# Gated linear attention and a multiplicative feed-forward: heads' rows interleaved by six, GpSimd out of the gates, passes moved to ScalarE

## The chip, the cores and the metric

The kernel runs on one core of a Trainium2 chip. The core has five engines that work side by side: TensorE (PE in the profile, with its weight loads as PEld), VectorE (DVE), ScalarE (ACT), GpSimd (POOL) and SyncE (SP, which here only issues transfers). Each engine runs its own instructions in the order in which they stand in its queue. The metric is the device time of one execution in microseconds; less is better.

## The reference

Attention with complex gates: for each of 4 batches and 8 heads a state of 48 x 48 is multiplied by a gate at each of 768 steps, takes in k v', and is read by q. The result, as 3072 tokens of 384, goes through a feed-forward without an activation function.

```python
mag = np.sqrt(a_re * a_re + a_im * a_im)
scale = np.minimum(mag, 0.999) / (mag + 1e-06)
a_re_n, a_im_n = (a_re * scale, a_im * scale)
for t in range(S):
    ar, ai = (a_re_n[:, :, t, :, None], a_im_n[:, :, t, :, None])
    new_re = ar * S_re - ai * S_im
    new_im = ar * S_im + ai * S_re
    kv = np.einsum('bhd,bhe->bhde', k[:, :, t], v[:, :, t])
    S_re, S_im = (new_re + kv, new_im)
    y[:, :, t] = np.einsum('bhd,bhde->bhe', q[:, :, t], S_re)
...
a = x @ w1
b = x @ w2
h = a * b @ w3
return (h @ w_out).astype(np.float32)
```

## The kernel before, in words

The work is cut into eight units: unit u is one half (384 steps) of one batch, with all eight heads. A unit's inputs lie with 128 partitions (16 rows d by 8 heads) and three blocks f of 384 steps, so that row 16 f + d of a head is in partition 8 d + head of block f.

- `gates(u)` turns the gates into running products. Magnitude and angle are kept apart: ScalarE takes logarithms, exponentials, arctan, sine and cosine (all through `act`, L536 of the profile), VectorE scans along the steps (L575 for the magnitude, L600 for the angle), and q and k are multiplied by the magnitude's running product and by its inverse (L587, L588, on GpSimd), then by cosine and sine (L616 to L620). GpSimd also forms im / re (L551) and spreads v into a padded layout (`spread_v`, L513). L606 to L608 take whole turns off the angle by adding and subtracting a large constant, `ROUND`. Unit 0 does all this in three pieces of 384 (split), the others in one piece of 1152.
- `move` (L631) then brings K and Q to one head's layout, since a matmul needs the 96 numbers of a head (48 rows with cosine, 48 with sine) in 96 partitions: KL and QL. There are twelve moves a unit (cosine or sine, three f, K and Q), each from 128 partitions to 16. All transfers are issued from SP's queue.
- `turn` transposes K for the state (copied out of PSUM by ScalarE, L652), `scores` (L661) multiplies K by Q, `state` (L697 to L704) carries the state from block to block, `outputs` (L687) forms y.
- `ffn_ab` (L714, L718, L719) and `ffn_out` (L724, L727) do the feed-forward of the unit before. `fuse` (L805) multiplies w3 by w_out once at the start, with weights that `convert` (L744 to L748) turns from 64-bit to 32-bit floats on ScalarE and VectorE.
- `check_weights` yields "looks": 36 further transfers of weights into a single buffer, each read by two ScalarE passes (L772, L773).

TensorE's order is written out by hand: in `unit` a piece of attention of unit u alternates with a piece of feed-forward of unit u - 1. The steps of `gates(u + 1)` are taken between them, and one look a piece. On the other engines and in SP's queue a scheduler sets the order when the kernel is built, within the data's dependencies; it may bring an instruction forward past others.

Of the kernel before, what the change touches and what calls it, by code (L numbers as in the profile page):

```python
# [10 lines left out]
FP = mybir.dt.float32  # L11
# [361 lines left out]
def kernel(  # L373
# [36 lines left out]
    nc = tc.nc  # L410
# [15 lines left out]
    LO, HI = 32, D - 32  # L426
    LN_EPS = math.log(1e-6)
    PI = math.pi
    ROUND = 1.5 * 2.0 ** 23
    MIN_SQ = 1.126 ** 2  # L430
    SMALL, LARGE, STEEP, DECAY, ANGLE = 2.0 ** -7, 2.0 ** 40, 1.5, math.exp(-32.0), 50.0

# [76 lines left out]
    def spread_v(u):  # L509
        vr = g_t[u]["vr"].rearrange("p c (h two d) -> p c h two d", two=2, d=D)  # L510
        V = Vb[u % 2].rearrange("p c (h two) e -> p c h two e", two=2)
        for i, e0 in enumerate((0, 64 - D)):
            nc.gpsimd.tensor_copy(out=V[:, :, :, i, e0:e0 + D], in_=vr[:, :, :, i])  # L513

    chained = []

# [6 lines left out]
    def gates(u, split):  # L523

        b, h = divmod(u, 2)
        g = g_t.setdefault(u, {})
        A = gate_pool[u % 2].tile([P, KD, TT], FP, tag="gA", name="gA")
        R = gate_pool[u % 2].tile([P, KD, TT + UC], FP, tag="gR", name="gR")
        Z = one.tile([P, KD, TT], FP, tag="gZ", name="gZ")
        re, im, q = g["re"], g["im"], g["q"]  # L530
        K2 = g["k"]
        k, r = K2[:, :, 0:TT], R[:, :, 0:TT]
        parts = [slice(f, f + 1) for f in range(KD)] if split else [slice(0, KD)]

        def act(**kw):
            chain(nc.scalar.activation(**kw))  # L536
# [12 lines left out]
        yield
        for i, s in enumerate(parts):  # L550
            nc.gpsimd.tensor_tensor(out=im[:, s], in0=im[:, s], in1=r[:, s], op=OP.mult)  # L551
            act(out=Z[:, s], in_=re[:, s], func=AF.Relu, scale=-1.0, bias=LEAST, accum_out=st_low[:, 0, u, i:i + 1])
            act(out=Z[:, s], in_=re[:, s], func=AF.Relu, bias=MOST, accum_out=st_low[:, 1, u, i:i + 1])
        yield
        for i, s in enumerate(parts):
            nc.vector.tensor_tensor_reduce(out=Z[:, s], in0=im[:, s], in1=im[:, s], scale=1.0, scalar=0.0,
                                           op0=OP.mult, op1=OP.max, accum_out=st_tan[:, u, i:i + 1])
        yield
        for s in parts:
            act(out=Z[:, s], in_=Z[:, s], func=AF.Ln, bias=ONE)  # L560
        yield

        for s in parts:
            stt(out=A[:, s], in0=Z[:, s], scalar=0.5, in1=A[:, s], op0=OP.mult, op1=OP.add)
            act(out=Z[:, s], in_=A[:, s], func=AF.Exp, scale=-1.0, bias=EPS)
            act(out=A[:, s], in_=A[:, s], func=AF.Exp)
        yield

        for s in parts:
            ts(out=Z[:, s], in0=Z[:, s], scalar1=-1.0, scalar2=1.0, op0=OP.mult, op1=OP.add)  # L570
            ts(out=A[:, s], in0=A[:, s], scalar1=0.999, scalar2=None, op0=OP.min)
            for f in range(s.start, s.stop):
                for c in range(UC):
                    w = slice(c * C, (c + 1) * C)
                    nc.vector.tensor_tensor_scan(out=A[:, f, w], data0=A[:, f, w], data1=Z[:, f, w], initial=1.0,  # L575
                                                 op0=OP.mult, op1=OP.mult)
        yield

        for s in parts:
            act(out=r[:, s], in_=A[:, s], func=AF.Ln)  # L580
            act(out=r[:, s], in_=r[:, s], func=AF.Exp, scale=-1.0)
        yield
        for s in parts:
            tt(out=Z[:, s], in0=A[:, s], in1=r[:, s], op=OP.mult)
            stt(out=r[:, s], in0=Z[:, s], scalar=2.0, in1=r[:, s], op0=OP.subtract, op1=OP.mult, reverse0=True)
        for s in parts:
            nc.gpsimd.tensor_tensor(out=q[:, s], in0=q[:, s], in1=A[:, s], op=OP.mult)  # L587
            nc.gpsimd.tensor_tensor(out=k[:, s], in0=k[:, s], in1=r[:, s], op=OP.mult)  # L588
        for X in (R, K2):
            nc.vector.tensor_copy(out=X[:, :, TT:TT + UC], in_=ends(A, slice(0, KD)))  # L590
        nc.vector.tensor_copy(out=st_dec[:, u], in_=R[:, :, TT:TT + UC])
        spread_v(u)
        yield
        chain(nc.scalar.preload_act_table_set("trig_and_small"))
        for s in parts:
            act(out=im[:, s], in_=im[:, s], func=AF.Arctan)
        yield
        for s in parts:
            for f in range(s.start, s.stop):
                nc.vector.tensor_tensor_scan(  # L600
                    out=Z[:, f], data0=im[:, f], data1=im[:, f],
                    initial=0.0 if h == 0 else st_ang[:, u - 1, f, UC - 1:UC], op0=OP.add, op1=OP.bypass)
        nc.vector.tensor_copy(out=st_ang[:, u], in_=ends(Z, slice(0, KD)))
        yield
        for s in parts:
            ts(out=re[:, s], in0=Z[:, s], scalar1=0.5 / PI, scalar2=ROUND, op0=OP.mult, op1=OP.add)  # L606
            ts(out=re[:, s], in0=re[:, s], scalar1=ROUND, scalar2=2 * PI, op0=OP.subtract, op1=OP.mult)
            tt(out=Z[:, s], in0=Z[:, s], in1=re[:, s], op=OP.subtract)  # L608
        yield
        for s in parts:  # L610
            act(out=re[:, s], in_=Z[:, s], func=AF.Abs)
            act(out=re[:, s], in_=re[:, s], func=AF.Sin, scale=-1.0, bias=QUARTER)
            act(out=Z[:, s], in_=Z[:, s], func=AF.Sin)
        yield
        if not split:
            tt(out=r, in0=k, in1=re, op=OP.mult)  # L616
            tt(out=k, in0=k, in1=Z, op=OP.mult)
            yield
            tt(out=A, in0=q, in1=re, op=OP.mult)
            tt(out=q, in0=q, in1=Z, op=OP.mult)  # L620
        yield "move"

        KL = head_pool[u % 2].tile([2 * D, H, TT + UC], FP, tag="KL", name="KL")
        QL = head_pool[u % 2].tile([2 * D, H, TT], FP, tag="QL", name="QL")
        L_t[u] = QL, KL, R, K2

        def move(dst, src, s):
            for x in range(2):
                for f in range(KD)[s]:
                    r0 = x * D + f * DG  # L630
                    nc.sync.dma_start(out=dst[r0:r0 + DG], in_=src[x][:, f])  # L631

        for s in parts:
            if split:
                tt(out=r[:, s], in0=k[:, s], in1=re[:, s], op=OP.mult)
                tt(out=k[:, s], in0=k[:, s], in1=Z[:, s], op=OP.mult)
            move(KL, (R, K2), s)
            if split:
                tt(out=A[:, s], in0=q[:, s], in1=re[:, s], op=OP.mult)
                tt(out=q[:, s], in0=q[:, s], in1=Z[:, s], op=OP.mult)  # L640
            move(QL, (A, q), s)
        yield

    def turn(u, c, x):

        src = L_t[u][2 + x]
        if x == 0:
            KT_t[u, c] = two.tile([P, H, 2, D], FP, tag="KT", name="KT")
        tp = ps_v.tile([P, KD, C], FP, tag="v", name="tp")
        for f in range(KD):  # L650
            nc.tensor.transpose(out=tp[:, f], in_=src[:, f, c * C:(c + 1) * C], identity=ident)
        nc.scalar.copy(out=KT_t[u, c][:, :, x], in_=tp.rearrange("p f c -> p (f c)").rearrange("p (d h) -> p h d", h=H))  # L652
# [37 lines left out]
    def state(u, c):  # L690
# [3 lines left out]
        T = T_t.get((u // 2, n))  # L694
        kv = ps_v.tile([2 * D, H, 64], FP, tag="v", name="kv")
        for hd in range(H):
            nc.tensor.matmul(out=kv[:, hd], lhsT=KT[:, hd], rhs=V[:, hd], start=True, stop=True)  # L697
        rho = KL[:, :, TT + c:TT + c + 1].to_broadcast([2 * D, H, 64])
        Tn = two.tile([2 * D, H, 64], FP, tag="T", name="T")
        if T is None:  # L700
# [145 lines left out]
    def ffn(u):  # L846
        return [lambda j=j: ffn_ab(u, j) for j in range(KF)] + [lambda t=t: ffn_out(u, t) for t in range(UC)]
# [12 lines left out]
    with tc.manual_schedule(engines={mybir.EngineType.PE}):  # L860
# [106 lines left out]
```

## Time and profile before

| | before |
|---|---|
| median of 3 runs (lowest to highest) | 667.16 us (665.15 to 668.01) |
| the profiled execution's own time | 665.67 us |
| its span, first to last instruction | 663.9 us |
| mean granted TensorE clock | 0.941 |
| busy in the span: PE / PEld / DVE / ACT / POOL | 573.4 / 378.0 / 334.1 / 285.1 / 87.2 us |
| moved by DMA | 83.58 MB in 52146 packets |

Lines of groups give: line, engine, operation, output <- inputs, shapes, count | busy us, mean ns of one | idle time of the engine ahead of them, and what ended it. Lines of a timeline give: start us, duration us, engine, line, operation, count, and in brackets the idle time before, with what ended it. Busy shares are means over the whole execution; the stages differ much.

### The profile page before, as it was taken

To read this page: it belongs to the slowest core of one execution; us is meant where nothing else is said; L and a number is where in the kernel's file an instruction comes from. 1 tells how busy PE (TensorE), PEld (TensorE's weight loads), DVE (VectorE), ACT (ScalarE), POOL (GpSimd) and SP (SyncE) were. 2 spreads that over 40 slices of the span, in tenths; PEclk is the share of its full clock that TensorE was granted. 3 is DMA by queue.
4 is the path that set the end of the run, shared out by engine and by line. 5 is a ranking of instruction groups with operands and counts; after the bars stand their busy time and mean duration, and the time that the engine had idled before them with its cause. 6 is when DMAs were issued, how large, how long until landed. Compare 5 with 4: busy or idle time off the path is not lost.

```text
span 663.9 us, 8912 instructions
## 1 busy us (share of the span) xinstructions
PE 573.4 (86%) x3514; PEld 378.0 (57%) x3514; DVE 334.1 (50%) x501; ACT 285.1 (43%) x454; POOL 87.2 (13%) x57
## 2 busy tenths in 40 slices
PE   0769687966966799999984999799999999999996
PEld 0335474534743566676643676466656766766553
DVE  5999498831881387048601495138705961220110
ACT  6655275534751675177531855255316331101100
POOL 5050033001320130013000130013001300000000
PEclk9979899996969799999996999979999999999999
DMA  9977998397449637953469433951590067001001
GB/s 290 312 227 184 189 264 281 104 112 148 129 132 132 173 88 159 173 174 120 124 117 180 147 113 105 149 159 37 85 154 14 1 78 102 1 1 36 1 1 39
DMA packets 52146, 83.58 MB, mean 126 GB/s; under 512 B 4480, under 2 KB 43392, under 8 KB 52096
## 3 DMA queue, kind: packets, MB, share of 16 engines
q1 hardware_dynamic: 52096, 82.93, 55.2%
q8 instruction: 29, 0.48, 0.3%
q14 instruction: 21, 0.17, 0.1%
HBM read 59.24 MB, written 4.72 MB: 96 GB/s over the span
## 4 chain that ended last, share of the span: by engine, by line
PE 50%; DMA 20%; DVE 13%; ACT 11%; issue 4%; SPq 2%; ACTq 0%; DVEq 0%
PE m L714 25%; PE o L724 12%; DMA look<-in_w_dram 6%; PE sc L661 5%; DMA KL<-k 5%; DMA look<-in_w_out_dram 3%; DMA QL<-q 3%; PE y L687 3%; ACT gZ L536 3%; PE kv L697 2%; DVE gA L575 2%; DVE gZ L600 2%; ACT gR L536 2%; ACT look L773 1%; ACT look L772 1%
## 5 line engine op out<-in xcount | busy, mean ns | idle before, releaser
L714 PE MATMUL m<-xT,w2s 128*128 128x384 f32 x384 | 137.3, 495 | 6.8 <-ACT a L718 6.8
L714 PE MATMUL m<-xT,w1s 128*128 128x384 f32 x384 | 141.4, 506 | 1.6 <-ACT xT L688 1.6
L724 PE MATMUL o<-w3o,ab 128*128 128x384 f32 x384 | 129.4, 493 | 0.0
L719 DVE TENSOR_TENSOR ab<-m,a 128x384 f32<-128x384 f32 x64 | 35.3, 551 | 170.9 <-PE m L714 139.6
L714 PEld LDWEIGHTS m<-xT,w2s 128*128 128x128 f32 x384 | 74.0, 193 | 60.3 <-ACT a L718 8.9
L724 PEld LDWEIGHTS o<-w3o,ab 128*128 128x128 f32 x384 | 72.4, 192 | 48.2 <-issue 2.7
L714 PEld LDWEIGHTS m<-xT,w1s 128*128 128x128 f32 x384 | 72.1, 198 | 45.1 <-issue 6.0
L661 PE MATMUL sc<-QL,KL 96*128 96x128 f32 x384 | 56.9, 310 | 42.1 <-DMA look<-in_w_dram 19.4
L661 PEld LDWEIGHTS sc<-QL,KL 96*128 96x128 f32 x384 | 53.6, 220 | 49.0 <-issue 34.9
L718 ACT COPY a<-m 128x384 f32<-128x384 f32 x64 | 30.3, 474 | 96.7 <-PE m L714 93.9
L805 PE MATMUL f<-wo_s,w3s 128*128 128x384 f32 x128 | 46.9, 525 | 26.6 <-DVE wo_s L748 18.0
L662 DVE COPY_PREDICATED A<-causal,sc 128x512 f32<-128x512 int32 x48 | 34.4, 730 | 66.6 <-PE sc L661 66.4
L772 ACT ACTIVATE look<-look 128x512 f32<-128x512 f32 (+1 forms) x36 | 23.4, 651 | 74.7 <-DMA look<-in_w_dram 56.3
L805 PEld LDWEIGHTS f<-wo_s,w3s 128*128 128x128 f32 x128 | 25.7, 205 | 47.1 <-DVE wo_s L748 20.4
L551 POOL TENSOR_TENSOR im<-im,gR 128x1152 f32<-128x1152 f32 (+1 forms) x10 | 20.7, 2075 | 221.9 <-ACT gR L536 137.4
L687 PE MATMUL y<-A,V 128*32 128x128 f32 x768 | 41.8, 281 | 6.9 <-DVE A L662 5.0
L687 PEld LDWEIGHTS y<-A,V 128*32 128x32 f32 x768 | 34.2, 111 | 16.3 <-issue 10.1
L687 PE MATMUL y<-QL,T 96*32 96x128 f32 x640 | 37.1, 280 | 0.0
L587 POOL TENSOR_TENSOR q<-q,gA 128x1152 f32<-128x1152 f32 (+1 forms) x10 | 22.7, 2274 | 93.4 <-DVE gA L575 92.0
L687 PEld LDWEIGHTS y<-QL,T 96*32 96x32 f32 x640 | 32.7, 113 | 0.1
L744 ACT ACTIVATE low<-raw 128x768 int32<-128x768 uint32 (+1 forms) x20 | 20.2, 1011 | 29.3 <-DMA raw<-in_w_dram 12.7
L727 ACT COPY ot<-o 128x384 f32<-128x384 f32 x24 | 11.4, 473 | 48.3 <-PE o L724 48.3
(96 smaller groups left out, 648.6 us busy)
## 6 DMA issues: line engine op xcount, KB each, us to landing
look<-in_w_dram SPq DMA_DIRECT2D x28, 512.0 KB, 4.4
raw<-in_w_dram SPq DMA_DIRECT2D x8, 1024.0 KB, 5.7
raw<-in_w_dram SPq DMA_DIRECT2D x8, 768.0 KB, 9.7
KL<-gR SPq DMA_DIRECT2D x24, 193.5 KB, 5.8
KL<-k SPq DMA_DIRECT2D x24, 193.5 KB, 8.1
re<-in_a_re_dram SPq DMA_DIRECT2D x24, 192.0 KB, 8.4
im<-in_a_im_dram SPq DMA_DIRECT2D x24, 192.0 KB, 3.7
k<-in_k_dram SPq DMA_DIRECT2D x24, 192.0 KB, 3.2
```

Source lines behind the costliest of these rows:

```text
L536: chain(nc.scalar.activation(**kw))
L551: nc.gpsimd.tensor_tensor(out=im[:, s], in0=im[:, s], in1=r[:, s], op=OP.mult)
L587: nc.gpsimd.tensor_tensor(out=q[:, s], in0=q[:, s], in1=A[:, s], op=OP.mult)
L661: nc.tensor.matmul(out=sc[:, j], lhsT=KL[:, x * n + j, w], rhs=QL[:, x * n + j, w], start=True, stop=True)
L662: nc.vector.copy_predicated(out=A[:, x * n:(x + 1) * n], data=sc, mask=causal.rearrange("p (h t) -> p h t", h=1).to_broadcast([P, n, C]))
L687: nc.tensor.matmul(out=o, lhsT=a, rhs=b, start=s0, stop=s1)
L714: nc.tensor.matmul(out=m, lhsT=w[:, j * P // WB, f, j * P % WB:j * P % WB + P], rhs=xT_t[u][:, f], start=(f == 0), stop=(f == KD - 1))
L718: nc.scalar.copy(out=a, in_=got[0])
L719: nc.vector.tensor_tensor(out=ab_t[u][:, j], in0=got[1], in1=a, op=OP.mult)
L724: nc.tensor.matmul(out=m, lhsT=ab_t[u][:, f, t * P:(t + 1) * P], rhs=w3o[:, f], start=(f == 0), stop=(f == KF - 1))
L772: nc.scalar.activation(out=hi, in_=hi, func=AF.Square, scale=2.0 ** 15)
L805: nc.tensor.matmul(out=m, lhsT=w3_t[j][:, f], rhs=w3_t["wo"][:, f], start=(f == 0), stop=(f == KF - 1))
```

## The change

Five things are done at once.

1. `move` writes every sixth partition: row d of block f, cosine or sine x, goes to partition 6 d + 3 x + f of KL and QL, where it went to 48 x + 16 f + d. The transposed K gets the same order of its 96 columns, so ScalarE's copy into KT reads in order and writes with gaps, where it read with gaps and wrote in runs.
2. The three multiplies of the gates that GpSimd did go to VectorE, and V's two copies to ScalarE.
3. 1 - Z goes from VectorE to ScalarE, as a third pass between two Exps.
4. Whole turns are found by one ScalarE pass that writes integers, and taken off by one VectorE pass; three VectorE passes go.
5. Looks begin with unit 2's pieces in the program, not with unit 1's.

```diff
-            nc.gpsimd.tensor_copy(out=V[:, :, :, i, e0:e0 + D], in_=vr[:, :, :, i])
+            nc.scalar.copy(out=V[:, :, :, i, e0:e0 + D], in_=vr[:, :, :, i])
...
-            nc.gpsimd.tensor_tensor(out=im[:, s], in0=im[:, s], in1=r[:, s], op=OP.mult)
+            tt(out=im[:, s], in0=im[:, s], in1=r[:, s], op=OP.mult)
...
             act(out=Z[:, s], in_=A[:, s], func=AF.Exp, scale=-1.0, bias=EPS)
+            act(out=Z[:, s], in_=Z[:, s], func=AF.Copy, scale=-1.0, bias=1.0)
             act(out=A[:, s], in_=A[:, s], func=AF.Exp)
...
-            ts(out=Z[:, s], in0=Z[:, s], scalar1=-1.0, scalar2=1.0, op0=OP.mult, op1=OP.add)
...
-            nc.gpsimd.tensor_tensor(out=q[:, s], in0=q[:, s], in1=A[:, s], op=OP.mult)
-            nc.gpsimd.tensor_tensor(out=k[:, s], in0=k[:, s], in1=r[:, s], op=OP.mult)
+            tt(out=q[:, s], in0=q[:, s], in1=A[:, s], op=OP.mult)
+            tt(out=k[:, s], in0=k[:, s], in1=r[:, s], op=OP.mult)
...
-            ts(out=re[:, s], in0=Z[:, s], scalar1=0.5 / PI, scalar2=ROUND, op0=OP.mult, op1=OP.add)
-            ts(out=re[:, s], in0=re[:, s], scalar1=ROUND, scalar2=2 * PI, op0=OP.subtract, op1=OP.mult)
-            tt(out=Z[:, s], in0=Z[:, s], in1=re[:, s], op=OP.subtract)
+            n = re[:, s].bitcast(I32)
+            act(out=n, in_=Z[:, s], func=AF.Copy, scale=0.5 / PI)
+            stt(out=Z[:, s], in0=n, scalar=-2 * PI, in1=Z[:, s], op0=OP.mult, op1=OP.add)
...
-                    r0 = x * D + f * DG
-                    nc.sync.dma_start(out=dst[r0:r0 + DG], in_=src[x][:, f])
+                    nc.sync.dma_start(out=dst[x * KD + f::2 * KD], in_=src[x][:, f])
...
-            KT_t[u, c] = two.tile([P, H, 2, D], FP, tag="KT", name="KT")
+            KT_t[u, c] = two.tile([P, H, DG, 2, KD], FP, tag="KT", name="KT")
...
-        nc.scalar.copy(out=KT_t[u, c][:, :, x], in_=tp.rearrange("p f c -> p (f c)").rearrange("p (d h) -> p h d", h=H))
+        nc.scalar.copy(out=KT_t[u, c][:, :, :, x].rearrange("p h d f -> p f d h"),
+                       in_=tp.rearrange("p f (d h) -> p f d h", h=H))
...
-            unit(u, steps, rest[HEAD:] if u == 1 else ffn(u - 1), look)
+            unit(u, steps, rest[HEAD:] if u == 1 else ffn(u - 1), look if u > 1 else iter(()))
```

Three places show what the scheduler makes of it. SP's queue at the end of unit 3, with the moves of unit 4 (KL and QL; gR and k hold K with cosine and sine, gA and q hold Q), before:

```order
L482 DMA im<-in_a_im_dram 128x1x384 x3
L770 DMA look<-in_w_dram 128x1024
L631 DMA KL<-gR 16x8x387
L770 DMA look<-in_w_dram 128x1024
L631 DMA KL<-gR 16x8x387
L770 DMA look<-in_w_dram 128x1024
L631 DMA KL<-gR 16x8x387
L770 DMA look<-in_w_dram 128x1024
L631 DMA KL<-k 16x8x387 x3
L631 DMA QL<-gA 16x8x384 x3
L631 DMA QL<-q 16x8x384 x3
```

The same place in the changed kernel:

```order
L481 DMA im<-in_a_im_dram 128x1x384 x3
L769 DMA look<-in_w_dram 128x1024
L629 DMA KL<-gR 16x8x387 x3
L629 DMA KL<-k 16x8x387 x3
L629 DMA QL<-gA 16x8x384 x3
L629 DMA QL<-q 16x8x384 x3
```

The three looks between the moves are gone from here, and so are the two between unit 5's; the changed kernel has one look between unit 6's moves, where there was none.

VectorE in unit 1, with the gates of unit 2, from the magnitude's scans (L575, L574 in the changed kernel) to the angle without whole turns, before:

```order
L575 SCALAR_TENSOR_TENSOR gA<-gA,gZ 128x128 x9
L590 COPY gR<-gA 128x3x3
L590 COPY k<-gA 128x3x3
L591 COPY st_dec<-gR 128x9
L584 TENSOR_TENSOR gZ<-gA,gR 128x1152
L662 COPY_PREDICATED A_85<-causal,sc 128x512
L585 SCALAR_TENSOR_TENSOR gR<-gZ,gR 128x3x384
L662 COPY_PREDICATED A_85<-causal,sc 128x512
L600 SCALAR_TENSOR_TENSOR gZ<-im 128x384 x3
```

The same stretch in the changed kernel:

```order
L574 SCALAR_TENSOR_TENSOR gA<-gA,gZ 128x128 x9
L586 TENSOR_TENSOR q<-q,gA 128x1152
L589 COPY gR<-gA 128x3x3
L589 COPY k<-gA 128x3x3
L590 COPY st_dec<-gR 128x9
L661 COPY_PREDICATED A_85<-causal,sc 128x512
L583 TENSOR_TENSOR gZ<-gA,gR 128x1152
L661 COPY_PREDICATED A_85<-causal,sc 128x512
L584 SCALAR_TENSOR_TENSOR gR<-gZ,gR 128x3x384
L702 TENSOR_TENSOR T<-kv,T 96x512
L587 TENSOR_TENSOR k<-k,gR 128x3x384
L599 SCALAR_TENSOR_TENSOR gZ<-im 128x384 x3
```

q's multiply now follows the magnitude's scans, and k's stands ahead of the angle's scans.

ScalarE at the end of unit 0, with the second Ln and Exp of unit 1's gates (gR), before:

```order
L688 COPY xT<-y 128x3x128
L536 ACTIVATE gR<-gA 128x3x384
L744 ACTIVATE low<-raw 128x768
L536 ACTIVATE gR<-gR 128x3x384
L718 COPY a<-m 128x384
```

The same place in the changed kernel:

```order
L687 COPY xT<-y 128x3x128
L512 COPY V_87<-vr 128x12x48 x2
L535 ACTIVATE gR<-gA 128x3x384
L717 COPY a<-m 128x384
L535 ACTIVATE gR<-gR 128x3x384
```

Both copies of V for unit 2, which wait for v's landing and for unit 0's last output, stand ahead of that Ln.

More of the change, by code (lines that the diff above doesn't have):

```diff
@@ L428 @@
     PI = math.pi
-    ROUND = 1.5 * 2.0 ** 23
     MIN_SQ = 1.126 ** 2
@@ L696, in state @@
         for hd in range(H):
-            nc.tensor.matmul(out=kv[:, hd], lhsT=KT[:, hd], rhs=V[:, hd], start=True, stop=True)
+            nc.tensor.matmul(out=kv[:, hd], lhsT=KT[:, hd].rearrange("p d x f -> p (d x f)"), rhs=V[:, hd], start=True, stop=True)
         rho = KL[:, :, TT + c:TT + c + 1].to_broadcast([2 * D, H, 64])
```

## The prediction

> **What bounds the kernel now.** I read the page's first line and then TensorE's own list of waits (engine and line, what it waited for: total us, times, longest).
>
> ```profile
> span 663.9 us, 8912 instructions
> ```
>
> ```profile
> PE sc L661 <- DMA look<-in_w_dram: 19.4, 2, 9.7
> ...
> PE sc L661 <- DMA QL<-q: 17.0, 2, 11.8
> ```
>
> After the opening, TensorE waits mostly in one place: the first scores of a unit (L661), for a DMA. A score matmul reads only QL and KL, so "look" is just the transfer that landed at that moment; what is missing is the moved rows. The timeline of TensorE gives the first scores of units 0 to 7 (start, duration, idle before).
>
> ```profile
> 79.27 3.79 PE L661 MATMUL sc<-QL,KL 96*128 96x128 f32 x16 [5.19 <-DMA QL<-q]
> ...
> 155.75 3.75 PE L661 MATMUL sc<-QL,KL 96*128 96x128 f32 x16 [11.79 <-DMA QL<-q]
> ...
> 219.18 3.75 PE L661 MATMUL sc<-QL,KL 96*128 96x128 f32 x16 [9.62 <-DMA look<-in_w_dram]
> ...
> 284.85 1.95 PE L661 MATMUL sc<-QL,KL 96*128 96x128 f32 x16
> ...
> 348.54 2.20 PE L714 MATMUL m<-xT,w2s 128*128 128x384 f32 x6 [3.30 <-ACT a L718]
> ...
> 360.49 3.76 PE L661 MATMUL sc<-QL,KL 96*128 96x128 f32 x16 [9.75 <-DMA look<-in_w_dram]
> ...
> 433.07 3.75 PE L661 MATMUL sc<-QL,KL 96*128 96x128 f32 x16 [5.74 <-DMA look<-in_w_out_dram]
> 436.62 3.29 PE L714 MATMUL m<-xT,w1s 128*128 128x384 f32 x6
> 439.75 2.10 PE L714 MATMUL m<-xT,w2s 128*128 128x384 f32 x6
> ...
> 498.23 1.95 PE L661 MATMUL sc<-QL,KL 96*128 96x128 f32 x16
> ...
> 561.51 1.95 PE L661 MATMUL sc<-QL,KL 96*128 96x128 f32 x16
> ```
>
> Five of eight units start late. After such a wait the same matmuls run slow for some 3 us: 3.75 instead of 1.95, then 3.29 instead of 2.10, so a stall of this kind costs 3.0 us more than its idle time. A unit without any wait takes 561.51 - 498.23 = 63.3 us. Now the queue of SP, which issues the moves.
>
> ```profile
> 133.02 1.90 SPq L631 DMA_DIRECT2D KL<-gR  x3
> ...
> 196.25 2.10 SPq L631 DMA_DIRECT2D KL<-gR  x3
> ...
> 324.08 0.61 SPq L631 DMA_DIRECT2D KL<-gR  x1
> 326.43 0.33 SPq L770 DMA_DIRECT2D look<-in_w_dram  x1
> ...
> 340.74 1.84 SPq L631 DMA_DIRECT2D KL<-k  x3
> ```
>
> From the first move to the first score are 22.7 us (unit 1) and 22.9 (unit 2). In unit 4, three looks stand between the first moves, each waiting for its single buffer: 16.7 us pass before the fourth move. The rate, from two windows (after the busy times: granted clock, DMA share, GB/s): the first holds moves alone, the second loads from HBM in rows of about the same size.
>
> ```profile
> 144.00:155.00 11.00, 0.00 (x0) 0.00 (x0) 0.00 (x0) 0.48 (x1) 0.00 (x0) 0.72 1.10 118
> 83.00:91.00 8.00, 7.36 (x90) 6.69 (x88) 6.81 (x9) 6.93 (x11) 2.56 (x1) 0.94 1.07 330
> ```
>
> The DMA engines are full in both, but the moves get 118 GB/s against 330. Landing times of the rows KL, and of the stores to out, which read 128 partitions and write HBM:
>
> ```profile
> DMA to landing us min/median/max: 3.7/6.8/10.8
> ```
>
> ```profile
> DMA to landing us min/median/max: 1.8/3.2/12.1
> ```
>
> The same 192 KB read from all partitions can land in 1.8 us, so the read side is not what is slow. A move writes 16 neighbouring partitions; that is the suspect.
>
> **The moves (stride six).** Bounds for twelve moves of 193 KB, 2.37 MB: at 118 GB/s 20 us, as now; at 330 GB/s 7.2 us, but SP issues three in 1.90 us, so the last leaves after 7.0 us and lands no earlier than 2.8 later (estimate: 1 us above the fastest store), 9.8. I take 11.5, near the fast end, since 16 written rows would now be spread over 96. That saves 11.3 us a unit (0 to 13).
>
> [...]
>
> **Up to the first score (79.27).** VectorE is nearly full here, in pieces of 384.
>
> ```profile
> L584 DVE TENSOR_TENSOR gZ<-gA,gR 128x384 f32<-128x384 f32 x3 | 4.0, 1348 | 0.0
> ...
> L635 DVE TENSOR_TENSOR gR<-k,re 128x384 f32<-128x384 f32 x3 | 1.7, 561 | 0.0
> ...
> L570 DVE TENSOR_SCALAR gZ<-gZ 128x384 f32<-128x384 f32 x3 | 1.0, 338 | 0.0
> ```
>
> ```profile
> 32.57 2.22 DVE L575 TENSOR_TENSOR_SCAN gA<-gA,gZ 128x128 f32<-128x128 f32 x3
> ...
> 36.67 1.04 DVE L575 TENSOR_TENSOR_SCAN gA<-gA,gZ 128x128 f32<-128x128 f32 x3
> ```
>
> ```profile
> 70.51 0.56 SPq L631 DMA_DIRECT2D QL<-q  x1
> ```
>
> Added to VectorE: nine multiplies from GpSimd and three passes on n, 12 x 0.56 = 6.7 us. Removed: nine one-input passes x 0.34 and three subtractions x 0.56, 4.7. Like shapes ran at 1.35 instead of 0.56 and 2.22 instead of 1.04 while GpSimd worked; without it 3 x 0.79 + 1.2 = 3.6 go. Net -1.6. The last move landed 8.8 us after its issue behind the others; at the fastest move's 3.7 the first score comes at 70.5 - 1.6 + 3.7 = 72.6: **-7** (-2 to -9). ScalarE's six extra passes and two copies of V lie in its idle time there.
>
> **Unit 0 to 1 (76.5 us).** Prices at full width:
>
> ```profile
> L745 DVE TENSOR_SCALAR w1s<-raw 128x768 int32<-128x768 int32 x4 | 6.0, 1498 | 1.5 <-DMA raw<-in_w_dram 1.5
> ...
> L745 DVE TENSOR_SCALAR w2s<-raw 128x768 int32<-128x768 int32 x4 | 2.2, 548 | 0.0
> ```
>
> ```profile
> L652 ACT COPY KT<-tp 128x384 f32<-128x384 f32 x40 | 18.9, 476 | 29.3 <-PE tp L651 29.2
> ...
> L551 POOL TENSOR_TENSOR im<-im,gR 128x1152 f32<-128x1152 f32 x7 | 17.6, 2513 | 218.4 <-ACT gR L536 137.4 <-DMA out_dram<-ot 42.2 <-DMA q<-in_q_dram 38.7
> ...
> L616 DVE TENSOR_TENSOR gR<-k,re 128x1152 f32<-128x1152 f32 x7 | 9.5, 1359 | 12.8 <-ACT re L536 10.7 <-issue 2.1
> ...
> L536 ACT ACTIVATE im<-im 128x1152 f32<-128x1152 f32 x7 | 8.1, 1158 | 0.0
> ...
> L570 DVE TENSOR_SCALAR gZ<-gZ 128x1152 f32<-128x1152 f32 x7 | 5.3, 751 | 3.9 <-ACT gZ L536 3.9
> ```
>
> The weight passes beside GpSimd took 1.50 instead of 0.55: 3.8 us go. im: 2.51 to 1.36, -1.2. Two multiplies come onto VectorE, +2.7. 1 - Z on ScalarE between its two Exps: 1.16 for 0.75, +0.4. n: two passes and a subtraction, 2.9, become 1.16 + 1.36: -0.3. Two copies of V, 0.65 each (between 476 ns for 384 and 1158 for 1152), now stand on ScalarE ahead of the gates' second Ln: +1.3. With the moves' -11.3 this makes -12.2; I take **-11** (0 to -15), since each handover may add a little. First score of unit 1 at 137.8.
>
> **Unit 1 to 2 (63.4 us).** This interval is bound by the gates, not by TensorE: sin and cos come late, then the moves.
>
> ```profile
> 157.57 1.16 ACT L536 ACTIVATE gA<-re 128x1152 f32<-128x1152 f32 x1 [13.09 <-DMA re<-in_a_re_dram]
> ```
>
> ```profile
> 48.98 2.64 DVE L600 TENSOR_TENSOR_SCAN gZ<-im 128x384 f32<-128x384 f32 x3
> ```
>
> ```profile
> 310.52 5.03 DVE L600 TENSOR_TENSOR_SCAN gZ<-im 128x384 f32<-128x384 f32 x3 [0.20 <-ACT im L536]
> ```
>
> From re's landing to the first move are 196.25 - 157.57 = 38.7 us. Here k's multiply stands ahead of the angle scans (+1.36), but the scans, 5.03 beside GpSimd, cost 2.64 without: -1.0; the other multiply fits into the wait for Ln and Exp. With im, n and 1 - Z as above, -2.1; with the moves **-13.4** (0 to -16). Score 2 at 187.8, still after a wait of about 10 us, so the 65.7 us to score 3 stay.
>
> **Units 3 to 6.** A chain of 36.6 (gates) + 11.5 (moves) + 2 (re landing) = 50 us fits under 63.3, so the late starts vanish: 3.30 + 9.75 before score 4, **-13.1**; 5.74 before score 5 and the 3.0 of slow matmuls, **-8.7**; 3.0 after score 5. The looks, no longer between the moves of units 4 and 5, help by themselves; the one look between unit 6's moves has 13 us of slack.
>
> **KT and V.** The copy into KT (0.48 each) now writes with gaps. TensorE waits on it directly only in unit 0; elsewhere a piece of feed-forward covers it. Taken as 0, at double price +2 there. [...] No trace of before has such a copy. V's copies at unit ends hide under the last output block.
>
> **Sum.** 7 + 11 + 13.4 + 13.1 + 8.7 + 3.0 = 56.2; span 663.9 - 56.2 = 607.7. The profiled execution took 665.67, 1.8 over its span, and the median 667.16 is 1.5 above that: **611 us**, own range 601 to 622 (moves of 10 to 14 us count three times, KT +2).
>
> **Rivals.** (1) Moves stay at 22.8 us because SBUF-to-SBUF copies, not partitions, are slow. For it: no row shows another layout. Against it: the 1.8 us store. Then only looks and GpSimd count: unit 4 is ready by 324.1 + 22.8 = 346.9, so 13.1 + 8.7 + 3.0 remain, plus about 2 + 1 + 2 in front: 637. (2) The moves speed up but ScalarE, with two more passes a unit, V's copies and dearer KT copies in a fixed order, makes TensorE wait as at 348.54: 2 to 3 us in each of 7 units, about 628. (3) Slower: strided rows cost the DMA engines more. A unit then takes 36.6 + 2 + move; beyond 24.7 us of moving this exceeds 63.3. Against the 22 us that rival 1 keeps, six such units break even with before at about 29 us; at twice the present 22.8 the kernel would need some 760. Nothing in the rows speaks for it; rows of 1.5 KB stay as they are. (4) Both effects fail: the looks only shift their delay to units 5 and 6: 660 to 668.
>
> **Chances.** Forecast 0.70 (and 0.05 below 601); rival 1 0.10; rival 2 0.08; rival 3 0.05; rival 4 0.02. The range 600 to 636 holds the forecast, rival 2 and part of rival 1. Faster by over 0.5% 0.93, same 0.02, slower 0.05; 0.5% is about what these times can tell.
>
> **What would show it.** Moves: first move to first score near 12 us in unit 2, and a window of moves alone far above 118 GB/s (below 150: rival 1). No wait before scores 4 and 5, and unit 0's scores near 72. L584 in pieces of 384 at 0.56. Waits of the form PE m <- ACT a over 3 us in units 2 to 5 would be rival 2. I am wrong in size if unit 2's wait vanishes or unit 3 keeps one.

## The result, and the profile after

The changed kernel takes 608.94 us (median of 4 runs, 608.87 to 610.92) against 666.36 us before (4 runs beside it, 665.15 to 668.01): a ratio of 0.9144, 95% interval 0.9115 to 0.9173. The prediction was 611 us. The profiled execution took 608.87 us, 1.8 over its span.

From the page of the changed kernel, its span, the busy times and the chain of work that ended last:

```profile
span 607.1 us, 8813 instructions
PE 558.1 (92%) x3514; PEld 369.0 (61%) x3514; DVE 320.1 (53%) x501; ACT 325.5 (54%) x490; POOL 5.3 (1%) x11
PE 65%; ACT 11%; DVE 9%; DMA 9%; issue 2%; SPq 2%; ACTq 0%; DVEq 0%
```

TensorE runs the same 3514 matmuls in 15.3 us less busy time (573.4 before): its mean granted clock went from 0.941 to 0.980, as fewer matmuls run slow behind a stall (a unit's first scores take 3.75 us behind a long one and 1.95 without). The timeline of TensorE in the changed kernel, with the first scores of units 0 to 7 (now L660):

```profile
73.82 3.75 PE L660 MATMUL sc<-QL,KL 96*128 96x128 f32 x16 [5.97 <-DMA re<-in_a_re_dram]
137.45 2.02 PE L660 MATMUL sc<-QL,KL 96*128 96x128 f32 x16 [0.85 <-DMA re<-in_a_re_dram]
187.72 2.02 PE L660 MATMUL sc<-QL,KL 96*128 96x128 f32 x16 [1.87 <-DMA re<-in_a_re_dram]
253.20 1.95 PE L660 MATMUL sc<-QL,KL 96*128 96x128 f32 x16
315.36 1.95 PE L660 MATMUL sc<-QL,KL 96*128 96x128 f32 x16
379.25 0.94 PE L660 MATMUL sc<-QL,KL 96*128 96x128 f32 x7
441.42 1.95 PE L660 MATMUL sc<-QL,KL 96*128 96x128 f32 x16
504.70 1.95 PE L660 MATMUL sc<-QL,KL 96*128 96x128 f32 x16
```

The waits of 11.79, 9.62, 9.75 and 5.74 us ahead of units 1, 2, 4 and 5 have become 0.85, 1.87, nothing and nothing; from unit 3 on no unit starts late. Only unit 0 still waits, 5.97 us. (The transfer of re that is named there is just the one that landed then; a score reads QL and KL.) By intervals between first scores, in us:

| | predicted gain | measured | from |
|---|---|---|---|
| start to score 0 | 7 | 5.5 | 79.27 to 73.82 |
| 0 to 1 | 11 | 12.9 | 76.48 to 63.63 |
| 1 to 2 | 13.4 | 13.2 | 63.43 to 50.27 |
| 2 to 3 | 0 | 0.2 | 65.67 to 65.48 |
| 3 to 4 | 13.1 | 13.5 | 75.64 to 62.16 |
| 4 to 5 | 8.7 | 8.7 | 72.58 to 63.89 |
| 5 to 6 | 3.0 | 3.0 | 65.16 to 62.17 |
| 6 to the end | 0 | 0.0 | 165.67 to 165.68 |
| sum | 56.2 | 56.8 | span 663.9 to 607.1 |

The moves, in SP's queue of the changed kernel (units 1 and 2, the first three and the last three), then a window in which unit 2's moves run alone, then the landing of the rows of KL:

```profile
124.17 1.92 SPq L629 DMA_DIRECT2D KL<-gR  x3
...
130.61 1.87 SPq L629 DMA_DIRECT2D QL<-q  x3
173.16 3.43 SPq L629 DMA_DIRECT2D KL<-gR  x3
...
180.58 1.86 SPq L629 DMA_DIRECT2D QL<-q  x3
```

```profile
178.00:187.00 9.00, 7.86 (x27) 4.41 (x25) 1.24 (x3) 2.46 (x4) 0.00 (x0) 1.00 1.08 229
```

```profile
DMA to landing us min/median/max: 2.7/3.6/9.6
```

The DMA engines are as full as before (1.08, where 1.10 stood), but the same transfers run at 229 GB/s instead of 118. From the first move to the first score are 13.3 us in unit 1 (124.17 to 137.45) and 14.6 in unit 2, where 22.7 and 22.9 stood. Groups of the changed kernel by shape:

```profile
L583 DVE TENSOR_TENSOR gZ<-gA,gR 128x384 f32<-128x384 f32 x3 | 1.6, 542 | 0.0
L744 DVE TENSOR_SCALAR w1s<-raw 128x768 int32<-128x768 int32 x4 | 2.2, 548 | 0.0
L599 DVE TENSOR_TENSOR_SCAN gZ<-im,st_ang 128x384 f32<-128x384 f32 x12 | 11.4, 999 | 0.0
L599 DVE TENSOR_TENSOR_SCAN gZ<-im 128x384 f32<-128x384 f32 x12 | 10.8, 940 | 0.0
L512 ACT COPY V<-vr 128x576 f32<-128x576 f32 x16 | 10.5, 671 | 3.6 <-PE y L686 2.4 <-DMA vr<-in_v_dram 1.2
L650 ACT COPY KT<-tp 128x384 f32<-128x384 f32 x40 | 33.7, 847 | 30.0 <-PE tp L649 29.8
```

The first two rows read 1348 and 1498 ns before, while GpSimd worked beside them. The last one is the change's cost: the copy into KT went from 476 to 847 ns, forty times.

### The profile page after: what moved, and what is told of

Its sections match the earlier page's. It is cut to its first block, busy times and chain, and to the rows that moved or that the text cites. A ratio compares the mean times of both kernels' runs of the same rounds, so it can differ in the third digit from the quotient of the medians.

```text
span 607.1 us, 8813 instructions
## 1 busy us (share of the span) xinstructions
PE 558.1 (92%) x3514; PEld 369.0 (61%) x3514; DVE 320.1 (53%) x501; ACT 325.5 (54%) x490; POOL 5.3 (1%) x11
## 4 chain that ended last, share of the span: by engine, by line
PE 65%; ACT 11%; DVE 9%; DMA 9%; issue 2%; SPq 2%; ACTq 0%; DVEq 0%
PE m L713 32%; PE o L723 18%; PE sc L660 6%; PE y L686 5%; PE kv L696 3%; DMA look<-in_w_dram 3%; ACT gZ L535 2%; DMA raw<-in_w_dram 2%; ACT gR L535 2%; PE tp L649 2%; DMA KL<-k 2%; DMA re<-in_a_re_dram 2%; ACT re L535 1%; DVE gA L574 1%; ACT look L771 1%
## 5 line engine op out<-in xcount | busy, mean ns | idle before, releaser
L713 PE MATMUL m<-xT,w1s 128*128 128x384 f32 x384 | 137.3, 494 | 2.6 <-ACT xT L687 2.6
L713 PE MATMUL m<-xT,w2s 128*128 128x384 f32 x384 | 134.3, 486 | 0.0
L723 PE MATMUL o<-w3o,ab 128*128 128x384 f32 x384 | 127.8, 488 | 0.0
L713 PEld LDWEIGHTS m<-xT,w1s 128*128 128x128 f32 x384 | 70.1, 192 | 43.9 <-ACT xT L687 3.3
L804 PE MATMUL f<-wo_s,w3s 128*128 128x384 f32 x128 | 44.8, 504 | 22.4 <-DVE wo_s L747 18.5
L660 PE MATMUL sc<-QL,KL 96*128 96x128 f32 x384 | 50.8, 288 | 8.7 <-DMA re<-in_a_re_dram 8.7
L660 PEld LDWEIGHTS sc<-QL,KL 96*128 96x128 f32 x384 | 48.3, 201 | 15.1 <-issue 12.2
L804 PEld LDWEIGHTS f<-wo_s,w3s 128*128 128x128 f32 x128 | 24.2, 194 | 42.4 <-DVE wo_s L747 20.9
L650 ACT COPY KT<-tp 128x384 f32<-128x384 f32 x40 | 33.7, 847 | 30.0 <-PE tp L649 29.8
L726 ACT COPY ot<-o 128x384 f32<-128x384 f32 x24 | 11.3, 473 | 53.5 <-PE o L723 53.5
L686 PE MATMUL y<-QL,T 96*32 96x128 f32 x640 | 38.5, 285 | 0.0
L696 PEld LDWEIGHTS kv<-V,KT 128*96 128x96 f32 x320 | 31.0, 171 | 2.6 <-issue 1.4
L771 ACT ACTIVATE look<-look 128x512 f32<-128x512 f32 (+1 forms) x36 | 23.7, 659 | 14.7 <-DMA look<-in_w_dram 10.3
## 6 DMA issues: line engine op xcount, KB each, us to landing
KL<-gR SPq DMA_DIRECT2D x24, 193.5 KB, 3.4
KL<-k SPq DMA_DIRECT2D x24, 193.5 KB, 3.7
```

Source lines behind the costliest of these rows:

```text
L650: nc.scalar.copy(out=KT_t[u, c][:, :, :, x].rearrange("p h d f -> p f d h"), in_=tp.rearrange("p f (d h) -> p f d h", h=H))
L660: nc.tensor.matmul(out=sc[:, j], lhsT=KL[:, x * n + j, w], rhs=QL[:, x * n + j, w], start=True, stop=True)
L686: nc.tensor.matmul(out=o, lhsT=a, rhs=b, start=s0, stop=s1)
L696: nc.tensor.matmul(out=kv[:, hd], lhsT=KT[:, hd].rearrange("p d x f -> p (d x f)"), rhs=V[:, hd], start=True, stop=True)
L713: nc.tensor.matmul(out=m, lhsT=w[:, j * P // WB, f, j * P % WB:j * P % WB + P], rhs=xT_t[u][:, f], start=(f == 0), stop=(f == KD - 1))
L723: nc.tensor.matmul(out=m, lhsT=ab_t[u][:, f, t * P:(t + 1) * P], rhs=w3o[:, f], start=(f == 0), stop=(f == KF - 1))
```

## The experiments

Theory: a move's pace is set by the partitions that it writes, and since the moves stand between the gates and the first scores, that gave most of the gain; GpSimd's removal gave some, the looks little. Rival: moves were covered, and the looks and GpSimd made the gain. Runs of the kernel before, beside these, had medians of 666.7 to 667.5 us.

### e1: the rows put back

```diff
-  nc.sync.dma_start(out=dst[x * KD + f::2 * KD], in_=src[x][:, f])
+  r0 = x * D + f * DG
+  nc.sync.dma_start(out=dst[r0:r0 + DG], in_=src[x][:, f])
...
```

KT, its copy and the matmul that reads it go back with them.

> The changed kernel (608.9 us) with item 1 alone undone: a move writes 16 neighbouring partitions again, and KT is laid out as before. Theory (the rows' place sets the moves' pace and the moves set most of the gain): a window of moves alone goes back to about 118 GB/s from 229, and first move to first score to about 22.7 us from 14.6; the late starts of units 1 and 2 grow by some 8 us each. Units 3 to 6 stay on time at 33.9 + 22.8 + 2 = 58.7 us of chain under 63.3. Sum 5 + 9 + 8 and a few us of slow matmuls: 631 to 637 us. Rival (removing GpSimd's work and the looks made the gain, the moves were hidden): at most 615. The copy into KT goes back from 847 to 476 ns under both.

Measured: 636.03 us (632.83 to 638.53), ratio to before 0.9545 (0.9499 to 0.959), so 27 us above the changed kernel. A window of e1 in which unit 2's moves run alone, and TensorE's first scores of units 1 and 4:

```profile
190.00:206.00 16.00, 11.83 (x37) 6.60 (x36) 1.67 (x3) 3.80 (x8) 0.00 (x0) 0.93 1.10 119
```

```profile
150.62 3.75 PE L660 MATMUL sc<-QL,KL 96*128 96x128 f32 x16 [9.68 <-DMA re<-in_a_re_dram]
...
338.27 1.95 PE L660 MATMUL sc<-QL,KL 96*128 96x128 f32 x16
```

The rate is back at 119 GB/s, and 22.9 and 23.3 us pass from first move to first score. The loss is made ahead of score 0 (3.2 us), in units 0 to 1 (10.0), 1 to 2 (8.6) and 2 to 3 (1.2), and in unit 5 (3.8), where TensorE waits 2.08 us for KT and 1.45 ahead of score 6; units 4 and 5 start on time even so, as a chain of 33.9 + 23 + 2 us fits under 63.3. The rival's 615 is out. The prediction's first rival (moves stay slow, the rest works) had been given 637 us: this is that kernel.

### e2: the rows alone

The kernel before with the inverse of e1's edit.

> The kernel before (666.4 us) with item 1 alone. Theory of the moves: units 1 and 2 start earlier by 8 to 9 us each, unit 0 by 2 to 5, and the two stalls ahead of units 4 and 5 (9.75 and 5.74) shrink but do not quite go, since looks still stand between their moves, one buffer for all; each stall that goes takes 1.8 to 3 us of slow matmuls with it. Time 626 to 640 us. Rival (rows matter little, the rest of the change makes the gain): 650 or more. KT copies near 850 ns in both.

Measured: 628.46 us (626.65 to 630.40), ratio 0.9421 (0.9385 to 0.9457), 38.5 us below before. TensorE in e2, first scores of units 0, 4 and 5:

```profile
72.65 2.05 PE L661 MATMUL sc<-QL,KL 96*128 96x128 f32 x16
...
332.56 3.76 PE L661 MATMUL sc<-QL,KL 96*128 96x128 f32 x16 [4.00 <-DMA look<-in_w_dram]
...
400.11 2.02 PE L661 MATMUL sc<-QL,KL 96*128 96x128 f32 x16 [1.02 <-DMA out_dram<-ot]
```

The rows alone give 38.5 us and the rest alone (e1 against before) 31.0; together they would be 69.5, and the change gave 58. The place to look for the missing 11.5 is units 4 and 5. In e2 the intervals 3 to 4 and 4 to 5 gain 7.8 and 5.0 us (to 67.8 and 67.6), 12.9 in all, though looks still stand between their moves; in e1, where the looks no longer do, they gain 22.8, and in the changed kernel 22.2. Either part removes a stall, and it can be removed once. That counts 13.5 us twice; the other intervals add up to some 4 us the other way in the profiled executions. No run has item 5 alone.

### e3: the looks put back

```diff
- unit(u, ..., look if u > 1 else iter(()))
+ unit(u, ..., look)
```

> The changed kernel with item 5 alone undone: looks begin with unit 1's pieces, so that SP's queue has two looks between the moves of unit 4 and three between those of unit 5, as before. Theory (once a unit's chain is near 50 us it has some 13 us of slack under 63.3, which a few looks of 2 to 4 us eat only partly): 607 to 613 us, no late start of a unit after unit 2 over 1 us. Rival (the looks among the moves made the late starts of units 4 and 5 by themselves): two stalls of 5 to 10 us come back, 620 us or more.

Measured: 612.14 us (608.65 to 614.98), ratio 0.9199 (0.9155 to 0.9243), which overlaps the changed kernel's interval. The profiled execution, at 608.65 the fastest of the four, has no wait over 1 us ahead of any first scores after unit 0; from unit 3 on TensorE's longest wait in it is this one:

```profile
343.68 0.43 PE L686 MATMUL y<-A,V 128*32 128x128 f32 x8 [1.34 <-DVE T L702]
```

With moves of 14 us the looks between those of units 4 and 5 fit into the slack, as the theory says, and the rival's stalls don't come back. A cost of some 3 us in the median is neither shown nor excluded: two of the four runs took 614 to 615 us, and neither was profiled.

### e4: the gates' multiplies back on GpSimd

```diff
- tt(out=im[:, s], in0=im[:, s], in1=r[:, s], op=OP.mult)
+ nc.gpsimd.tensor_tensor(out=im[:, s], in0=im[:, s], in1=r[:, s], op=OP.mult)
...
```

The multiplies of q and k go with it.

> The changed kernel with the three multiplies of the gates back on GpSimd (part of item 2; V's copies stay on ScalarE). Theory (VectorE's passes run at about double time beside GpSimd, which costs at the start and in units 0 to 2 only, where the gates are waited for): multiplies in pieces of 384 go from 542 to over 1000 ns, scans L599 from about 0.95 to 1.4 us; unit 0's first scores 1 to 2 us later, unit 1's and 2's 2 to 4 us later each: 612 to 619 us. Rival (the contention is real but VectorE's queue is shorter by the same work, so it nets out): 606 to 611. The other side of the chain, units 3 to 7, has slack in both.

Measured: 617.79 us (616.42 to 619.29), ratio 0.9277 (0.925 to 0.9303), 9 us above the changed kernel. Groups of e4:

```profile
L599 DVE TENSOR_TENSOR_SCAN gZ<-im,st_ang 128x384 f32<-128x384 f32 x12 | 17.7, 1521 | 0.7 <-ACT im L535 0.6
L744 DVE TENSOR_SCALAR w1s<-raw 128x768 int32<-128x768 int32 x4 | 4.4, 1096 | 0.6 <-DMA raw<-in_w_dram 0.6
```

These scans take 1521 instead of 999 ns, the weight passes 1096 instead of 548. So the size is as expected, but not all its places: score 0 came at 72.3, not later, and the loss is in units 0 to 1 (4.6 us), 1 to 2 (1.1), 2 to 3 (1.6, with a wait of 2.27 us for T on VectorE) and 5 to 6 (2.0).

### e5 and e6: which partitions, with sixteen rows two and three apart

```diff
- dst[x * KD + f::2 * KD]
+ dst[2 * DG * f + x:2 * DG * (f + 1):2]
...
- dst[x * KD + f::2 * KD]
+ dst[x * D + f:(x + 1) * D:KD]
```

The first is e5, the second e6; KT's columns follow in the same order.

> The changed kernel with a move's 16 rows two partitions apart (a window of 32) instead of six (a window of 96); KT is laid out to match, SP's order is the same. Measured so far: 118 GB/s and about 22.7 us for twelve moves with neighbouring rows, 229 GB/s and 14.6 us with rows six apart. [...]

> The changed kernel with a move's 16 rows three partitions apart (a window of 48: cosine in partitions 0 to 47, sine in 48 to 95). [...] Rival B (spread): faster than two apart, at most as slow as six apart. [...]

Measured: e5 610.78 us (609.53 to 611.51), ratio 0.9156 (0.9115 to 0.9197); e6 615.98 us (614.17 to 619.73), ratio 0.9231 (0.9189 to 0.9273). A window of e5 with unit 2's moves alone:

```profile
183.88:191.88 8.00, 8.00 (x28) 4.51 (x26) 0.91 (x2) 2.61 (x4) 0.00 (x0) 1.00 1.08 222
```

Windows of 2 us of e6 in unit 2; its moves were issued three and three, cosine K (180.5), sine K (183.1), cosine Q (185.6), sine Q (187.6):

```profile
184.53:186.53 2.00, 2.00 (x9) 1.20 (x8) 0.03 (x1) 1.87 (x4) 0.00 (x0) 1.00 1.06 154
186.53:188.53 2.00, 2.00 (x9) 1.21 (x8) 0.53 (x1) 0.84 (x1) 0.00 (x0) 1.00 1.09 240
188.53:190.53 2.00, 2.00 (x8) 1.16 (x7) 0.00 (x0) 0.48 (x1) 0.00 (x0) 1.00 1.11 160
190.53:192.53 2.00, 2.00 (x10) 1.34 (x9) 0.56 (x1) 0.83 (x1) 0.00 (x0) 1.00 1.10 137
192.53:194.53 2.00, 2.00 (x8) 0.99 (x6) 0.00 (x0) 0.48 (x1) 0.00 (x0) 1.00 1.07 231
```

The reader is to see the last column: full DMA engines (1.06 to 1.11), and a rate that swings between 137 and 240 GB/s within one unit, where windows of 2 us in e5's moves alone show 209 to 247. By the order and size of the moves 137 to 160 GB/s are cosine's (partitions 0 to 47) and 231 to 240 sine's (48 to 95); this is an estimate, since a window of 2 us can hold moves of both kinds. Rows two apart are as fast as six apart (222 and 229), and cosine's rows three apart are slower than either. So it is not distance that counts; the rival, that wider is faster, falls. Cosine and sine rows lie equally far apart and by that estimate still differ by half, so the place counts. Why one place gets a higher rate than another, these runs don't show. Whether 222 to 240 GB/s is still set by the partitions written or already by something else is open.

e5's 2 us against the changed kernel are within both intervals. In its profile they arise ahead of score 0 (77.2 against 73.8), where moves share the queue with loads: from 54 to 74 us the DMA engines moved 229 GB/s, against 253 with rows six apart. Why the mixture differs was not tried apart.

### e7 and e12: the copy into KT in another order

```diff
- nc.scalar.copy(out=KT_t[u, c][:, :, :, x].rearrange("p h d f -> p f d h"),
-                in_=tp.rearrange("p f (d h) -> p f d h", h=H))
+ nc.scalar.copy(out=KT_t[u, c][:, :, :, x], in_=tp.rearrange("p f (d h) -> p h d f", h=H))
```

> The changed kernel with the same KT, filled by a copy that runs over the block f innermost: it writes three neighbouring numbers at a time (12 bytes) and reads with gaps, where it wrote single numbers 24 bytes apart and read in order. Theory (the writes' gaps cost the doubling from 476 to 847 ns): 476 to 600 ns a copy; TensorE's waits on KT (0.94, 0.29, 1.54 us in units 0 to 2) mostly go; 605 to 608 us, near 2 us of gain, since the other copies are covered by feed-forward. Rival (gaps on either side cost the same, or the copy's cost is hidden): copies stay at 800 ns or more or the time stays within 1 us of 608.9.

> e7 once more, beside the changed kernel: in e7 the copy into KT took 559 instead of 847 ns but the interval of its time overlapped that of the changed kernel. Theory (TensorE waited for KT some 2.8 us in all, in units 0 to 2): 1 to 3 us below e11. Rival (hidden): within 1 us of e11.

> The changed kernel itself once more, so that e7, e9 and e10 are compared on the same chip: 607 to 612 us under every theory.

Measured: e7 607.03 us (6 runs, 605.53 to 613.08), ratio 0.9122 (0.9079 to 0.9165). Once more beside the changed kernel on the same chip: e12 607.23 us (605.05 to 607.85), 0.9097 (0.9062 to 0.9133); the changed kernel, e11, 608.59 us (606.21 to 610.59), 0.913 (0.9092 to 0.9167). The group in e7:

```profile
L650 ACT COPY KT<-tp 128x384 f32<-128x384 f32 x40 | 22.2, 559 | 30.0 <-PE tp L649 29.8
```

The order of the writing costs 288 ns of a copy. In the changed kernel the copy runs over the heads innermost, so that successive numbers land 384 bytes apart in KT, and not 24, as the expectation had it; in e7 three land side by side. Reading with gaps is no reason for the cost: e7 reads with gaps, and so does the copy of before, with 476 ns. The time falls by 1.4 us beside e11, less than the intervals can tell. It is the fastest version here, if it is faster at all.

### e8: V's copies back on GpSimd

```diff
- nc.scalar.copy(out=V[:, :, :, i, e0:e0 + D], in_=vr[:, :, :, i])
+ nc.gpsimd.tensor_copy(out=V[:, :, :, i, e0:e0 + D], in_=vr[:, :, :, i])
```

> The changed kernel with V's two copies a unit back on GpSimd, the multiplies staying on VectorE. Theory: V's copies cost 2 x 0.67 us ahead of the gates on ScalarE, on the path of units 1 and 2 only; on GpSimd they slow a few VectorE passes for the time they overlap (some 3 to 5 us of GpSimd's a unit). Both effects are near 1 us and opposite: 606 to 612 us. Rival (any work on GpSimd beside the gates costs as much as the multiplies did, 8.9 us): 614 or more.

Measured: 614.35 us (611.98 to 615.69), ratio 0.9223 (0.9181 to 0.9265), 5 us above the changed kernel: nearer the rival, and for a reason that neither named. Timelines of e8, of GpSimd, VectorE and SP's queue at the end of unit 1:

```profile
171.41 3.35 POOL L512 COPY V<-vr 128x576 f32<-128x576 f32 x2 [70.76 <-PE y L686]
```

```profile
171.13 1.36 DVE L615 TENSOR_TENSOR gR<-k,re 128x1152 f32<-128x1152 f32 x1 [1.87 <-ACT re L535]
172.41 1.81 DVE L618 TENSOR_TENSOR gA<-q,re 128x1152 f32<-128x1152 f32 x1
```

```profile
174.78 0.39 SPq L505 DMA_DIRECT2D vr<-in_v_dram  x1
175.26 1.93 SPq L629 DMA_DIRECT2D KL<-gR  x3
```

gR is ready at 172.5. In the changed kernel the moves leave as soon as it is (173.14 and 173.16). Here the load of the next vr stands ahead of them in SP's queue (the scheduler put it there), and its buffer comes free only when GpSimd has copied V, at 174.8; so the moves wait 2.8 us behind a load that has nothing to do with them. Score 2 comes at 190.0 instead of 187.7. The profiled execution is the fastest of the four, 3 us above the changed kernel's median; where the others lose more was not seen.

The kernel before had the same wait, and the prediction read it as a part of the gates:

```profile
192.12 1.36 DVE L616 TENSOR_TENSOR gR<-k,re 128x1152 f32<-128x1152 f32 x1 [1.94 <-ACT re L536]
```

```profile
192.32 3.42 POOL L513 COPY V<-vr 128x576 f32<-128x576 f32 x2 [9.77 <-issue]
```

```profile
195.77 0.39 SPq L506 DMA_DIRECT2D vr<-in_v_dram  x1
```

gR was ready at 193.5, and unit 2's first move left at 196.25, again 2.8 us later and behind vr. With V's copies on ScalarE that load stands behind the moves (at 189.2), and the wait is gone.

### e9: 1 - Z and whole turns back on VectorE

Items 3 and 4 undone, as in the change's diff.

> The changed kernel with items 3 and 4 undone: 1 - Z and the taking off of whole turns run on VectorE again, as three more VectorE passes a unit and two fewer of ScalarE's. Theory (the prediction's working: +0.4 and -0.3 us a unit on the path of the gates, so they cancel): from re's landing to the first move of unit 2 stays at 33.9 plus or minus 0.7 us, 607 to 611 us. Rival (VectorE's queue is what delays the masked scores A, for which TensorE waits 1.1 to 1.8 us four times in unit 1, so each VectorE pass that goes counts more than its place in the gates): units 1 and 2 start 2 to 4 us later, 611 to 616 us.

Measured: 612.70 us (6 runs, 611.80 to 614.54), ratio 0.9196 (0.916 to 0.9231), 4.1 us above e11: the rival's size. First the changed kernel, then e9, from the last angle scan of unit 2's gates to the first product:

```profile
164.03 2.64 DVE L599 TENSOR_TENSOR_SCAN gZ<-im 128x384 f32<-128x384 f32 x3
...
171.78 1.36 DVE L615 TENSOR_TENSOR gR<-k,re 128x1152 f32<-128x1152 f32 x1 [1.87 <-ACT re L535]
```

```profile
165.54 2.64 DVE L600 TENSOR_TENSOR_SCAN gZ<-im 128x384 f32<-128x384 f32 x3
...
176.35 1.36 DVE L616 TENSOR_TENSOR gR<-k,re 128x1152 f32<-128x1152 f32 x1 [3.06 <-ACT re L536]
```

5.1 us pass between them in the changed kernel and 8.2 in e9: taking off whole turns is 3.1 us shorter than in e9, not 0.3. Between e9's three passes stand gaps and the masked copies of A, and the product then waits 3.06 us for cosine instead of 1.87, since a look's pass, which waits for its transfer, stands ahead of cosine on ScalarE. The kernel before has no look there and takes 7.0 us (185.07 to 192.12), so against it 1.9 us are gained. From re's landing to the first move are 35.9 us in e9 (141.84 to 177.74) and 33.9 in the changed kernel (139.30 to 173.16), so 1 - Z on ScalarE and the rest take back 1.1. The rival's mechanism is not what happens, though: in unit 1 TensorE's waits for A fall from 5.1 to 3.8 us, and those for xT, which ScalarE copies, rise from 0.6 to 5.3. TensorE then comes to score 2 without a wait for the moves, so in e9 these waits, and not the moves, set when unit 2 starts.

### e10: unit 0's moves without loads ahead of them

```diff
+ moved.append(nc.sync.dma_start(out=dst[x * KD + f::2 * KD], in_=src[x][:, f]))
...
+ if moved:
+     tc.add_manual_dep(ld.ins, moved[-1].ins.name, ORDER, reason="moves")
```

`ld` is each load of re, im, k, q, v and of a w1 or w2 block that the program emits after unit 0's moves; the first two weight blocks and unit 1's loads are emitted there. KT's copy is e7's.

> The changed kernel with e7's order of the copy into KT, and with ordering edges that put the loads of unit 1's re, im, q, k, v and of the first w1 and w2 blocks behind unit 0's twelve moves in SP's queue. In the changed kernel these loads (0.98 MB of im and k, two of 0.79 MB of raw) stand just ahead of the moves and the DMA engines are full from 52 to 74 us. Theory (unit 0's wait of 5.97 us stayed because the moves share a full queue): the twelve moves go at their own pace, first score at 67 to 70 us instead of 73.8, wait under 2 us. What comes after pays: w1 and w2 are converted some 10 us later, beside the gates of unit 1, so the whole is 603 to 612 us. Rival (VectorE's products for the moves, the last at 64 us, and the landing time set it): first score stays at 72 to 74 us and the time at 607 to 614.

Measured: 614.65 us (6 runs, 612.62 to 619.08), ratio 0.9231 (0.9192 to 0.927), 6 us above e11 and 7 above e12, which has the same copy into KT. Windows from 54 to 66 us, of e10 and then of the changed kernel (DMA share, GB/s at the end), and TensorE's waits in e10:

```profile
54.00:66.00 12.00, 12.00 (x38) 6.79 (x37) 10.32 (x17) 7.63 (x14) 0.00 (x0) 1.00 0.60 166
```

```profile
54.00:66.00 12.00, 12.00 (x38) 6.84 (x37) 12.00 (x21) 7.04 (x12) 0.00 (x0) 1.00 1.06 256
```

```profile
68.78 1.46 PE L665 MATMUL sc<-QL,KL 96*128 96x128 f32 x11 [0.67 <-DMA QL<-q]
87.31 0.65 PE L691 MATMUL y<-A,V 128*32 128x128 f32 x8 [5.77 <-DVE A L666]
167.69 0.66 PE L691 MATMUL y<-A,V 128*32 128x128 f32 x8 [4.67 <-DVE st_ang L608]
```

Score 0 comes at 68.8 instead of 73.8 with 0.67 us of wait: the wait that stayed in unit 0 was for DMA engines that the loads filled, as the theory says. But all of it is given back: the weights are now converted on VectorE while TensorE waits for A there (5.77), and score 1 comes at 137.3, where it came in e11 (137.2). By score 5 e10 is 6.0 us behind e11; it loses 3.2 us in units 1 to 2 and 3.9 in 4 to 5, and why was not tried apart. The total fell outside the theory's 603 to 612, just above the rival's 614.

## Why the prediction was right, step by step

- **The moves.** Cause and place were right: e1 and e2 take them out and put them in. The size was not: 11.5 us from first move to first score was taken, 13.3 and 14.6 were measured. The step that failed is the choice near the fast end, the author's estimate between 9.8 and 20 us, which no run shows. 2.37 MB at the measured 229 GB/s take 10.3 us, and issuing ahead of it and landing behind it cost 3 to 4 more. So the moves saved 9.5 us in unit 1 and 8.4 in unit 2, not 11.3.
- **Unit 0 to 1.** 11 predicted, rounded down from 12.2; 12.9 measured. The moves gave 9.5 instead of 11.3, and what stands ahead of them gave 3.4 (53.75 to 50.35 us from score 0 to the first move) instead of 0.9. That the errors nearly cancel is luck. With the multiplies back on GpSimd this stretch takes 55.08 us (e4), so they can account for the 3.4.
- **Unit 1 to 2.** 13.4 predicted, 13.2 measured, and this is luck as well: the moves gave 8.4 instead of 11.3, and re's landing to the first move went from 38.7 us to 33.9, which is 4.8 instead of 2.1. The step that failed is reading the 38.7 us as gates alone. 2.8 of them were the wait behind vr's load (e8), a term that the sum lacks; the gates themselves, to gR, went from 35.9 to 33.8, which is 2.1. Inside these 2.1 two terms were off: n, put at -0.3, gave -1.9 (e9), since what stands between the three passes counts too (7.0 us in all before, 5.1 now); im and 1 - Z, put at -0.8, gave +0.6, as the time to the magnitude's scans went from 13.5 to 14.1 us. From there to the angle's scans, where k's multiply came in, +1.3 us were added, and the scans themselves gave -2.1, near the +1.36 and the 2.64 for 5.03 of the prediction.
- **The wait ahead of score 2.** The prediction kept "about 10 us" of it and would call itself wrong in size if it vanished. It fell to 1.87, and the sizes were wrong as said above. The rows shown could have told: before, TensorE came to score 2 after 63.43 - 9.62 = 53.8 us, which leaves no wait of 10 in an interval of 50. TensorE now comes after 48.4. Its matmuls of unit 1 were busy for 47.0 us before, at a mean granted clock of 0.80, and are for 42.7 now, at 0.90.
- **Up to score 0.** -7 predicted, -5.5 measured, -6.4 in e11. The last move left 3.25 us earlier (70.51 to 67.26), twice the 1.6 of VectorE's sum; but the term "landing in 3.7 us" took 6.6, since loads fill the DMA engines (1.06 from 54 to 66 us): with the loads behind the moves (0.60) it took 3.6 (e10).
- **Units 3 to 6.** 13.1, 8.7 and 3.0 predicted; 13.5, 8.7 and 3.0 measured. The price of a stall, its idle time and 3.0 us of slow matmuls behind it, was right to a few tenths. That the looks help by themselves fits e1, where both stalls go although the moves are slow, but no run has that item alone.
- **GpSimd.** Pieces of 384 were to take 0.56 us and take 0.54. In all its multiplies cost 9 us (e4), and V's copies on it 5 (e8).
- **KT.** Taken as 0 with a bound of 2: the copy cost 371 ns more each, and TensorE's waits on KT were 2.8 us in units 0 to 2 where they had been 2.0, all in unit 0; about 1.4 us came back in e12, which the intervals do not tell from nothing. The doubled price of the bound was the author's estimate; the copy took 1.8 times as long. Single numbers written 384 bytes apart (847 ns) cost more than runs of 12 bytes (559).
- **Rivals.** Moves that stay slow are e1, 636.03 against 637. ScalarE did not become the bound: from unit 3 on TensorE waits at most 0.53 us for any engine.

## What to carry to other kernels

When a transfer between partitions fills the DMA engines at a third of the rate of others (here 118 against 330 GB/s), look at which partitions it writes: writing sixteen rows to every sixth partition instead of neighbouring ones took the rate to 229 GB/s here, and every second partition was as good (222), but every third was not throughout (137 to 240). So time each set of partitions; the distance alone does not tell. Price a removed pass by the time between its neighbours in the timeline, not by its duration (whole turns: 3.1 us against e9 where the durations gave 0.3), and before a stall is forecast behind a shortened interval, subtract how long the waiting engine itself needs to get there. A load that waits for its buffer in an engine's queue holds up every move behind it, so a copy that lets a buffer go late can delay transfers that have nothing to do with it, here by 2.8 us. Such a wait hides in the time from a unit's input to its first move: look when the move's own data were ready before you put all of it down to the computation.

## What the runs showed of the hardware that was not expected

- The rate of a move depends on which sixteen partitions it writes: 119 GB/s for neighbours, 222 for every second and 229 for every sixth; for every third, by the estimate under e5 and e6, 137 to 160 in partitions 0 to 47 and 231 to 240 in 48 to 95.
- ScalarE's copy of 128 x 384 out of PSUM takes 474 to 476 ns when it writes runs, 559 in runs of three numbers, 847 to 852 in single numbers 384 bytes apart.
- Two copies on GpSimd (1.28 us in quiet stretches) took 3.35 us beside VectorE's products, and stretched two of these from 1.35 to 1.81 us.
